# Tail scores of two pairs of heads in four 64x64 tiles, with a new order of the work: a fused attention and mixer kernel

## The chip, the core and the metric

The kernel runs on one core of one Trainium2 chip. Its time is device microseconds of one execution; the median of three runs of the kernel before is 616.5 us (616.19 to 616.97). Engines are named as in the profile: PE (TensorE matmul), PEld (its weight loads), DVE (VectorE), ACT (ScalarE), POOL (GpSimd) and SP (here the queue that issues the DMAs).

## The reference

Attention with rotary position embedding over 4 batches, 8 heads, 576 positions and 64 numbers per head, and then an MLP mixer on the result, all in float32:

```
q_rot, k_rot = rotate(q), rotate(k)
scores = matmul(q_rot, k_rot.T) / sqrt(64);  scores -= max(scores)
attn = exp(scores);  attn /= sum(attn) + 1e-9
x = matmul(attn, v), heads side by side              # (4, 576, 512)
u = x + (relu(x.T @ w_tok1) @ w_tok2).T              # mixing over the 576 positions
out = u + relu(u @ w_ch1) @ w_ch2                    # mixing over the 512 channels
```

The four mixer weights are float64 in memory.

## The kernel before

**Attention** goes pair by pair: 16 pairs of heads of one batch. 576 positions are 4 blocks of 128 and a tail of 64. `prep(n)` loads k, q and v of a pair (SP), rotates k and q (L339 to L345, on POOL; for the first pair on DVE), transposes them in 64x64 pieces on PE (L373) and copies them out of PSUM (L384). `pair(n)` takes the query blocks in `ORDER = [0, 1, None, 2, 3]`, where `None` is the tail. Per block of 128 queries:

- L467: scores of both heads, each as a 64x128 tile of PE (head 0 on rows 0 to 63, head 1 on rows 64 to 127, side by side), in two halves of 288 keys. A float32 matmul makes two records in the profile, so one half of one block is four records.
- L418: DVE scales the scores into SBUF and keeps the running extreme; L422: ACT takes the exponential over 576 keys and its sum.
- L490: PE transposes the probabilities, L495 copies them to `pt` (on ACT or DVE, as the planner finds; two copies per head).
- L508: after two blocks, probabilities times v, as two 128x64 column tiles; 256 columns for blocks 0 and 1, 320 for blocks 2, 3 and the tail. L511 copies it out, L537 transposes it back, L542 and L546 divide by the sums into X.

The **tail** of a pair has 64 queries for each of two heads. `prep` writes them as the two diagonal blocks of a 128x128 operand `bd` (L395, two POOL copies per pair; the rest of `bd` is zero), and L437 multiplies all 128 rows of k with it, in the whole array. Its sums stand in column R of `l`; L520 moves half of them to the lower partitions, L523 adds 1e-9 (POOL) and L526 inverts (DVE).

**Mixer weights** are turned from float64 into pairs of float32 parts by `f64_split` (L577 to L598), a chain that goes ACT, DVE, ACT, with some steps on DVE or POOL as the planner finds. `tokens(b)` splits X into two parts (L659, L661) and mixes the positions of batch b (first weights L679, relu L684 and L687, second weights L701, sum L704). Batch 0 is mixed inside the attention program, batches 1 to 3 in `mixers`. Then X is transposed (L770, L775, L776), and `cm1` (L796) and `cm2` (L819, sum L821) mix the channels in 4 groups of 5 chunks; the last sums go to memory.

**The order** of the work is not the order of the code. Every step is a `Task` of a `Plan` with an engine (or two to choose from), a guessed duration, what it needs, the buffers it holds and a priority. `Plan.run` gives each engine again and again the ready task with the lowest priority among those that could start within `SLACK` of the earliest; a task with two engines takes the one where it would end first. Priorities are 9 per pair plus the numbers of the table `AT`; `LAG` is the time from the end of a task to the start of one that needs it. The hardware sees only the order that comes out, with semaphores.

Of the kernel before, what the change touches and what calls it, by code (L numbers as in the profile page):

```python
# [65 lines left out]
class Task:  # L66
    __slots__ = ("alts", "deps", "bufs", "prio", "end", "eng", "waits", "heirs", "mode", "port", "lag")


LAG = {"PE": 0.2, "ACT": 0.14, "DVE": 0.12, "POOL": 0.12, "SP": 1.8}  # L70


class Plan:


    def __init__(self):
        self.tasks = []
        self.clock = {e: 0.0 for e in LAG}
        self.slack = SLACK
        self.mode = None  # L80

    def add(self, eng, dur, fn, deps=(), bufs=(), prio=0.0, alts=(), mode="full", port=False, lag=0.0):
        t = Task()
        t.mode = mode
        t.port = port
        t.lag = lag
# [38 lines left out]
    def run(self):  # L125
# [10 lines left out]
        while left:  # L136
            best = {}
            for t in ready:
                c = None
                for eng, dur, fn in t.alts:  # L140
# [4 lines left out]
                    if c is None or s + dur < c[0]:  # L145
                        c = (s + dur, s, eng, dur, fn)
# [3 lines left out]
            for eng, lst in best.items():  # L150
                first = min(x[0] for x in lst)
                x = min((x for x in lst if x[0] <= first + self.slack[eng]), key=lambda x: (x[1], x[0]))
                if pick is None or x[0] < pick[0]:
                    pick = x
            assert pick, "no task can start"
            t, (end, s, eng, dur, fn) = pick[2], pick[3]
# [36 lines left out]
AT = {'load': [-311.48, -308.58, -58.96], 'rot': [1889.94, -216.09], 'pt': [-100.67, -63.74], 'bd': [-253.52], 'qk': [14.66, 1777.02, -290.55, -143.73, -330.56, -75.94, -278.36, -253.03, -71.25, -216.26], 'mx': [28.88, 15.51, -498.29, -196.51, -331.08, 1812.6, -110.88, -411.67, -437.32, 1660.53, -65.25, 1592.69, -438.98, -224.08, -437.26, 1980.9, -38.01, -303.7, -400.95, -14.52], 'ex': [-299.71, 1566.3, 1763.5, 33.52, -329.21, -34.07, -105.55, -415.73, 1706.66, -38.02], 'tr': [23.38, -74.36, -44.78, 1659.9, -10.24, -95.08, 2000.17, 1899.59, -435.89, -250.66], 'cp': [-408.04, -310.8, -118.02, -449.87, -264.03, -245.16, -436.72, -414.97, -25.86, -38.07], 'pv': [1795.8, -117.48], 'p1': [1768.03, -101.8], 'fin': [2001.36], 'tok': [-4.78, 1596.11, -550.18, 17.36, 1868.43, 1586.91], 'inv': [1863.98], 'f6': [1766.06], 'tk': [11.25, 1893.27, -116.2, -80.72]}  # L193
EARLY = 1
FIRST = -60.0
SWITCH = 0.15
SLACK = {'PE': 0.018, 'ACT': 0.047, 'DVE': 0.002, 'POOL': 0.109, 'SP': 0.028}
# [18 lines left out]
def pool(n):  # L216
    return n * 0.00235 + 0.08
# [3 lines left out]
def rope_attention_mixer_kernel(ctx: ExitStack, tc: tile.TileContext, q, k, v, w_tok1, w_tok2, w_ch1, w_ch2, tab, out):  # L221
# [37 lines left out]
    def attention(ctx):  # L259
# [12 lines left out]
        bds = slots("bd", 3, [P, P])  # L272
# [4 lines left out]
        ls = slots("l", 4, [P, R + 1, 2])  # L277
        ris = slots("ri", 3, [P, R + 1, 2])
# [20 lines left out]
        ready, ready_v, bd_of = {}, {}, {}  # L299
# [5 lines left out]
        def prep(n):  # L305
            b, hp = divmod(n, HP)
            pos = 9 * n
            for nm, src, pr in (("k", k, 0.0), ("q", q, 0.5), ("v", v, 1.0)):
# [13 lines left out]

                pl = pos + AT["load"][int(2 * pr)]
                rows = ((0, 2), (2, R)) if n == 0 and nm == "k" else ((0, R),)
                l = [add("SP", 0.5, ld(*x), bufs=[rb], prio=pl) for x in rows]
                l += [add("SP", 0.65, (ldv if nm == "v" else ldt)(o), bufs=[rb], prio=pl) for o in range(2)]
# [26 lines left out]
                for r0, r1 in parts:  # L353
                    if r0:
                        x = x + l[1:]
                    for i in range(4):
# [4 lines left out]
                        else:  # L361
                            x = [add("POOL", pool(w * (z1 - z0) // (R + 1)), rot(nc.gpsimd, i, r0=z0, r1=z1), x, bufs, pos + AT["rot"][int(2 * pr)])
# [26 lines left out]
                if nm == "q":  # L389
                    bb = Buf(bds)  # L390
                    bdone = []
                    pp = pos + AT["bd"][0]
                    for h in range(2):
# [3 lines left out]
                    bd_of[n] = (bdone, bb)  # L397

        ORDER = [0, 1, None, 2, 3]
        W2 = S // 2  # L400

        def pair(n):
            b, hp = divmod(n, HP)
            lb = Buf(ls)
            pt = [Buf(pts) for _ in range(2)]
# [506 lines left out]
```

## Time and profile before

| | |
|---|---|
| median of three runs | 616.5 us (616.19 to 616.97) |
| profiled execution, span from the first to the last instruction | 614.2 us |
| what lies outside the span, against the median | 2.3 us |
| PE busy | 596.1 us, 97% |
| DVE, ACT, POOL busy | 439.8, 304.8, 220.0 us |
| granted PE clock | 1.00 |

The profiled execution has no time of its own beside its span, so the span is compared with the median. Read it in stages: up to 13 us the first operands arrive; from 13 to 265 us attention runs (PE, DVE, ACT and POOL all busy); from 265 to 312 us positions are mixed; from 312 us on channels are mixed, where PE goes on almost without a gap.

### The profile page before, as it was taken

The numbers are of one execution on the slowest core, as the hardware profiler recorded it, in microseconds if no ns is written. First come the engines' busy times: TensorE is split into PE (matmuls) and PEld (weight loads), VectorE is DVE, ScalarE is ACT, GpSimd is POOL, SyncE is SP. The second block draws the span as 40 slices with busy tenths as digits, with TensorE's granted clock in tenths as the row PEclk, the third lists the DMA queues.
The fourth block names the chain that finished last, engine by engine and source line by source line (L and its number), as shares of the span: only waits on it lengthen the run. The fifth ranks groups of instructions, "written<-read, shape, count | busy, mean of one in ns | idle before, by whom it ended". The sixth has DMA issues, their size and how long they took to land.

```text
span 614.2 us, 12749 instructions
## 1 busy us (share of the span) xinstructions
PE 596.1 (97%) x4752; PEld 465.6 (76%) x4752; DVE 439.8 (72%) x1243; ACT 304.8 (50%) x769; POOL 220.0 (36%) x347
## 2 busy tenths in 40 slices
PE   4999999999999999998999999999999999999997
PEld 3777777777677777766788888888888888888885
DVE  6899999999999999389779895388334943223232
ACT  2988998999788888435235542144102411011110
POOL 3989979888899710235221020001000000000000
PEclk9999999999999999999999999999999999999999
DMA  5622332323221020002122320042001200001123
GB/s 156 184 66 82 85 99 64 99 72 82 67 65 42 25 70 2 2 27 60 35 60 69 115 75 27 1 128 78 0 1 34 70 1 0 1 0 69 68 69 102
DMA packets 33676, 36.13 MB, mean 59 GB/s; under 512 B 13776, under 2 KB 27088, under 8 KB 33616
## 3 DMA queue, kind: packets, MB, share of 16 engines
q1 hardware_dynamic: 32784, 35.01, 19.7%
q8 instruction: 37, 0.61, 0.4%
q10 hardware_dynamic: 832, 0.33, 0.2%
q14 instruction: 23, 0.19, 0.1%
HBM read 30.61 MB, written 4.72 MB: 58 GB/s over the span
## 4 chain that ended last, share of the span: by engine, by line
PE 90%; DVE 6%; DMA 1%; ACT 1%; issue 1%; ACTq 0%; POOL 0%; DVEq 0%; SPq 0%; POOLq 0%
PE m L796 24%; PE m L819 24%; PE s L508 11%; PE s L467 10%; PE s L490 6%; PE m L701 3%; PE s L437 3%; PE m L679 2%; PE s L373 2%; DVE p L418 1%; PE s L701 1%; PE s L679 1%; PE s L447 1%; PE s L537 1%; DVE xs L661 1%
## 5 line engine op out<-in xcount | busy, mean ns | idle before, releaser
L798 ACT ACTIVATE gh<-m 128x512 fp32r<-128x512 f32 (+1 forms) x60 | 33.3, 555 | 173.9 <-PE m L796 173.6
L422 ACT ACTIVATE p<-p,nm 128x576 f32<-128x576 f32 x128 | 98.4, 772 | 18.8 <-DVE p L418 18.3
L800 DVE SCALAR_TENSOR_TENSOR gl<-m,gh 128x512 fp32r<-128x512 f32 (+1 forms) x60 | 38.3, 638 | 70.0 <-ACT gh L798 69.6
L796 PE MATMUL m<-uh,c1h 128*128 128x512 f32 (+1 forms) x240 | 88.4, 368 | 0.0
L796 PE MATMUL m<-ul,c1h 128*128 128x512 f32 (+1 forms) x240 | 88.3, 368 | 0.0
L796 PE MATMUL m<-uh,c1l 128*128 128x512 f32 (+1 forms) x240 | 88.3, 368 | 0.0
L821 DVE TENSOR_TENSOR X<-m,X 128x512 f32<-128x512 f32 x64 | 44.2, 690 | 57.6 <-PE m L819 57.1
L508 PE MATMUL s<-pt,vraw 128*64 128x256 f32 (+1 forms) x640 | 84.8, 411 | 0.0
L819 PE MATMUL m<-c2h,gh 128*128 128x512 f32 x216 | 84.2, 390 | 0.0
L819 PE MATMUL m<-c2l,gh 128*128 128x512 f32 x216 | 84.1, 389 | 0.0
L819 PE MATMUL m<-c2h,gl 128*128 128x512 f32 x216 | 84.0, 389 | 0.0
L467 PE MATMUL s<-kt,qt 64*128 64x288 f32 x512 | 82.7, 430 | 1.0 <-DVE qt L384 0.7
L508 PEld LDWEIGHTS s<-pt,vraw 128*64 128x64 f32 x640 | 43.6, 137 | 32.3 <-DVE p L418 2.3
L589 POOL TENSOR_TENSOR fa<-fc,fa 128x384 f32<-128x384 f32 (+3 forms) x13 | 13.3, 1020 | 138.6 <-DVE fa L587 138.6
L418 DVE TENSOR_SCALAR_CACHE_REDUCE p<-s,nm 128x288 f32<-128x288 f32 x128 | 61.2, 511 | 0.5 <-PE s L467 0.3
L490 PEld LDWEIGHTS s<-ident,p 64*128 64x128 f32 x1152 | 48.7, 139 | 14.5 <-issue 4.5
L467 PEld LDWEIGHTS s<-kt,qt 64*128 64x128 f32 x512 | 50.5, 192 | 9.8 <-DVE p L418 1.7
L490 PE MATMUL s<-ident,p 64*128 64x64 f32 x1152 | 55.0, 226 | 0.9 <-DVE oT L511 0.4
L418 DVE TENSOR_SCALAR_CACHE_REDUCE p<-s 128x288 f32<-128x288 f32 x128 | 53.3, 450 | 2.2 <-PE s L467 1.9
L495 ACT COPY pt<-s 128x320 f32<-128x320 f32 (+1 forms) x146 | 52.0, 411 | 4.4 <-PE s L490 3.6
L796 PEld LDWEIGHTS m<-ul,c1h 128*128 128x128 f32 x240 | 45.2, 189 | 7.7
L796 PEld LDWEIGHTS m<-uh,c1h 128*128 128x128 f32 x240 | 45.2, 188 | 7.7
(135 smaller groups left out, 1080.5 us busy)
## 6 DMA issues: line engine op xcount, KB each, us to landing
stg<-in_moe_w_ch_dram SPq DMA_DIRECT2D x16, 384.0 KB, 3.2
stg<-in_moe_w_ch_dram SPq DMA_DIRECT2D x12, 512.0 KB, 3.7
qraw<-in_q_dram SPq DMA_DIRECT2D x16, 256.0 KB, 2.9
vraw<-in_v_dram SPq DMA_DIRECT2D x16, 256.0 KB, 2.8
out_dram<-X SPq DMA_DIRECT2D x16, 256.0 KB, 2.3
kraw<-in_k_dram SPq DMA_DIRECT2D x15, 256.0 KB, 2.8
stg<-in_moe_w_tok_dram SPq DMA_DIRECT2D x4, 512.0 KB, 4.4
kraw<-in_k_dram SPq DMA_DIRECT2D x32, 32.0 KB, 2.6
```

Source lines behind the costliest of these rows:

```text
L418: return lambda: nc.vector.tensor_scalar(out=p()[:, c * W2:(c + 1) * W2], in0=sb.t[:, 0:W2], scalar1=-D ** -0.5, scalar2=nm.t[:, 0:1] if c ...
L422: return lambda: nc.scalar.activation(out=p(), in_=p(), func=ACTF.Exp, bias=nm.t[:, 1:2], scale=-1.0, accum_out=l())
L467: nc.tensor.matmul(sbs[h].t[:, 0:W2], flat(qt.t)[halves[h], TL + j * P:TL + (j + 1) * P], flat(kt.t)[halves[h], TL * (1 - h) + u * W2:TL * ...
L490: nc.tensor.transpose(xy[z].t[:, i * TL:(i + 1) * TL], pb.t[halves[z], c0:c0 + P], ident[halves[z], halves[z]])
L495: return lambda: e(out=pt[c].t[:, R * h:R * h + m, o + z * TL:o + (z + 1) * TL], in_=xy[z].t[:, 0:m * TL].rearrange("p (r s) -> p r s", r=m))
L508: nc.tensor.matmul(ab.t[halves[h], 0:w], vb.t[:, h, r, :], m, start=(r == 0), stop=(r == R))
L701: nc.tensor.matmul(tb.t[0:w], a, m, start=(i == 0), stop=(i == 5))
L796: nc.tensor.matmul(tb.t[:, 0:n], a, m, start=(i == 0), stop=(i == len(lst) - 1))
L798: x = add("ACT", act(n), lambda f=f, tb=tb: nc.scalar.activation(out=gb.t[0][:, f, 0:n], in_=tb.t[:, 0:n], func=ACTF.Relu), [x], [tb, gb], ...
L800: y = add("DVE", dve(n), lambda f=f, tb=tb: nc.vector.scalar_tensor_tensor(out=gb.t[1][:, f, 0:n], in0=tb.t[:, 0:n], scalar=0.0, in1=gb.t[ ...
L819: nc.tensor.matmul(tb.t, a, m, start=(i == 0), stop=(i == len(lst) - 1))
L821: y = add("DVE", 0.69, lambda u=u, tb=tb: nc.vector.tensor_tensor(out=u, in0=tb.t, in1=u, op=ALU.add), [z] + sums.get((ci, x), []), [tb], ...
```

## The change

- **Tail scores.** `bd` and its copies are gone. `tails(n)` does the tails of two pairs n and n+1 (n even) together: four matmuls of 64 rows by 64 columns, each on its own quarter of the array (64 queries of one head of one pair against 288 keys), in a fourth mode `quad` beside row, col and full. Head h goes to PSUM bank h, so one bank holds the two pairs' queries of one head. The tails stand fourth in the even pair and not at all in the odd one: `ORDER = ([0, 1, 2, None, 3], [0, 1, 2, 3])`.
- **What hangs on it.** The odd pair's tail columns go with its blocks 0 and 1, so its 320 wide product is the first and not the second. Tail sums have their own small tiles: `l` shrinks to 8 columns, one copy (L463), one addition (L464) and one reciprocal (L465) per two pairs come in for the tails, the copy L520 per pair goes.
- **The planner's numbers.** `LAG` gets new values and `PAIR` values by pair of engines; a choice between two engines adds `BIAS` (0.08 for DVE, -0.51 for POOL) to the end; priorities differ for even and odd pairs; `AT` and `SLACK` are new, also for the mixing of positions.
- **Smaller edits.** The first q is loaded in two parts like the first k; the splits of two row blocks of batch 1 move into the attention program (`PRE`); the last block's second product and sum go in two halves of 256 columns, each with its own DMAs out.

The core of the diff (the table `AT` is all new, two entries stand for it):

```diff
-LAG = {"PE": 0.2, "ACT": 0.14, "DVE": 0.12, "POOL": 0.12, "SP": 1.8}
+LAG = {"PE": 0.2, "ACT": 0.15, "DVE": 0.14, "POOL": 0.2, "SP": 2.4}
+PAIR = {("PE", "DVE"): 0.27, ("DVE", "PE"): 0.175, ("DVE", "ACT"): 0.115, ("ACT", "PE"): 0.16, ("POOL", "PE"): 0.52}
...
-                    if c is None or s + dur < c[0]:
-                        c = (s + dur, s, eng, dur, fn)
+                    key = s + dur + BIAS.get(eng, 0.0)
+                    if c is None or key < c[0]:
+                        c = (key, s, eng, dur, fn)
...
-AT = {..., 'pv': [1795.8, -117.48], ...}
+AT = {..., 'pv': [-52.61, -86.6, -9.66, -21.02], ...}
+PRE = 2
+BIAS = {'DVE': 0.08256, 'POOL': -0.51382}
...
-                        def cp(h=h, tb=tb, bb=bb):
-                            nc.gpsimd.tensor_copy(out=bb.t[halves[h], halves[h]], in_=tb.t[halves[h], 2 * R + 1])
-                        bdone.append(add("POOL", 0.3, cp, done, [bb, tb], pp))
...
-        ORDER = [0, 1, None, 2, 3]
+        ORDER = ([0, 1, 2, None, 3], [0, 1, 2, 3])
...
+                def qk(sbs=sbs, u=u):
+                    for x in range(2):
+                        for h in range(2):
+                            nc.tensor.matmul(sbs[h].t[halves[x ^ h], 0:W2], flat(qt[x].t)[halves[h], 2 * R * TL + TL:2 * R * TL + 2 * TL],
+                                             flat(kt[x].t)[halves[h], TL + u * W2:TL + (u + 1) * W2], start=True, stop=True)
+                x = add("PE", 0.485, qk, kd + qd + [x[0] for x in t], [*sbs, *kt, *qt, *nms_, *pbs], g + AT["qk"][2 * i + u], mode="quad")
...
-                            nc.tensor.matmul(sb.t[:, 0:W2], bb.t, flat(kt.t)[:, TL + u * W2:TL + (u + 1) * W2], start=True, stop=True)
-                        t = add("PE", 0.485, qk, bdone + kd + [t], [sb, bb, kt, nm, pb], g + AT["qk"][2 * i + u])
...
-                w = 2 * P + (TL if c == 1 else 0)
-                c0 = 2 * P * c
+                w = 2 * P + (TL if c != odd else 0)
+                c0 = c * (2 * P + odd * TL)
...
+                last = g == NG - 1 and ci == NC - 1 and x == len(chunks[ci]) - 1
+                w = DM // (2 if last else 1)
...
+            splits(EARLY, range(PRE), 9 * 4 * (EARLY + 1) + AT["pre"][0])
```

What comes out of the planner is shown at three places.

PE, in the middle of attention, before: from the transposes of one pair to its tail scores (L437) and its first product with v (L508).

```order
L490 MATMUL s<-ident,p_116 128x64 x18
L447 MATMUL s<-ident,pq_119 128x64 x10
L467 MATMUL s<-kt_109,qt_111 128x288 x8
L537 MATMUL s<-ident,oT_124 128x64 x10
L437 MATMUL s<-kt_109,bd_114 128x288 x2
L508 MATMUL s<-pt_123,vraw_103 64x256 x10
L373 MATMUL s<-ident,uk_105 128x64 x10
```

The same place in the changed kernel: L425 are the tail scores of two pairs, L502 and L525 the scores and transposes of blocks, L543 the product with v.

```order
L525 MATMUL s<-ident,p_112 128x64 x8
L425 MATMUL s<-kt_108,qt_110 64x288 x2
L425 MATMUL s<-kt_109,qt_111 64x288 x2
L425 MATMUL s<-kt_108,qt_110 64x288 x2
L425 MATMUL s<-kt_109,qt_111 64x288 x2
L525 MATMUL s<-ident,p_112 128x64 x10
L502 MATMUL s<-kt_108,qt_110 128x288 x2
L502 MATMUL s<-kt_109,qt_111 128x288 x4
L502 MATMUL s<-kt_108,qt_110 128x288 x2
L525 MATMUL s<-ident,p_113 128x64 x8
L543 MATMUL s<-pt_120,vraw_104 64x256 x10
```

Two full-array matmuls in each pair, most often right ahead of a product with v, became eight small ones in every second pair, both halves in one run between transposes; k and q of both pairs have to be there for them.

POOL, before, from the last rotation (L345): L395 the last copies for `bd`, L598 a low part of the position weights (the last step of `f64_split`; L589 and L591 are its product and sum), L523 additions to the sums, L661 splits of X.

```order
L345 TENSOR_TENSOR uq_106<-uq_106,w_107 128x6x32
L395 COPY bd_112<-qt_111 64x64 x2
L598 TENSOR_TENSOR w2l<-fh_70,w2h 128x512
L523 TENSOR_SCALAR l_128<-l_128 128x10
L523 TENSOR_SCALAR l_129<-l_129 128x10
L523 TENSOR_SCALAR l_130<-l_130 128x10
L661 TENSOR_TENSOR xs_87<-X_60,xs_87 128x512
L661 TENSOR_TENSOR xs_88<-X_60,xs_88 128x512
```

POOL in the changed kernel, from its last rotation (L352): L626, L628 and L635 are product, sum and low part, L555 and L464 the additions to the sums.

```order
L352 TENSOR_TENSOR uq_106<-uq_106,w_107 128x6x32
L628 TENSOR_TENSOR fh_70<-fh_70,fa_68 128x512
L555 TENSOR_SCALAR l_125<-l_125 128x8
L635 TENSOR_TENSOR w1l<-fh_69,w1h 128x512
L635 TENSOR_TENSOR w1l<-fh_70,w1h 128x512
L464 TENSOR_SCALAR lt_132<-lt_132 64x4
L555 TENSOR_SCALAR l_126<-l_126 128x8
L626 TENSOR_TENSOR fa_67<-fc,fa_67 128x256
L628 TENSOR_TENSOR fh_69<-fh_69,fa_67 128x256
L626 TENSOR_TENSOR fa_68<-fc,fa_68 128x512
L628 TENSOR_TENSOR fh_70<-fh_70,fa_68 128x512
L635 TENSOR_TENSOR w2l<-fh_70,w2h 128x512
```

Before, one 512 wide step of the position weights stood here and most others on DVE, in the middle of attention; now six stand in these rows, and two more in the next eight.

PE, in the mixing of positions, before: the first weights of batch 2 (L679), all second weights of batch 1 (L701), then the first weights of batch 2 again.

```order
L679 MATMUL m_4127<-xs_88,w1h 128x512 x2
L679 MATMUL m_4127<-xs_88,w1l 128x512
L701 MATMUL m_4121<-rs,w2h 128x512 x2
L701 MATMUL m_4121<-rs,w2l 128x512
L701 MATMUL m_4121<-rs,w2h 128x512 x2
L701 MATMUL m_4121<-rs,w2l 128x512
L701 MATMUL m_4122<-rs,w2h 128x512 x2
L701 MATMUL m_4122<-rs,w2l 128x512
```

The same place in the changed kernel: L724 are first weights, L746 second weights.

```order
L746 MATMUL m_4130<-rs,w2h 128x512 x2
L746 MATMUL m_4130<-rs,w2l 128x512
L724 MATMUL m_4134<-xs_88,w1h 128x512 x2
L724 MATMUL m_4134<-xs_88,w1l 128x512
L724 MATMUL m_4135<-xs_88,w1h 128x512 x2
L724 MATMUL m_4135<-xs_88,w1l 128x512
L724 MATMUL m_4134<-xs_87,w1h 128x512 x2
L724 MATMUL m_4134<-xs_87,w1l 128x512
L724 MATMUL m_4135<-xs_87,w1h 128x512 x2
L724 MATMUL m_4135<-xs_87,w1l 128x512
L746 MATMUL m_4131<-rs,w2h 128x512 x2
L746 MATMUL m_4131<-rs,w2l 128x512
```

Second weights of one batch and first weights of the next now alternate.

## Rows read from the trace of the kernel before

**Rows 1.** The page's parts 1 and 4: busy time; the chain by engine.

```profile
PE 596.1 (97%) x4752; PEld 465.6 (76%) x4752; DVE 439.8 (72%) x1243; ACT 304.8 (50%) x769; POOL 220.0 (36%) x347
...
PE 90%; DVE 6%; DMA 1%; ACT 1%; issue 1%; ACTq 0%; POOL 0%; DVEq 0%; SPq 0%; POOLq 0%
```

**Rows 2.** Stages: us, PE, PEld, DVE, ACT, POOL busy (instructions), clock, DMA share, GB/s.

```profile
13.00:265.00 252.00, 249.37 (x3042) 179.49 (x3038) 230.66 (x859) 210.04 (x590) 185.16 (x298) 1.00 0.25 69
265.00:312.00 47.00, 44.27 (x239) 33.70 (x240) 38.79 (x66) 16.91 (x32) 16.35 (x12) 1.00 0.14 40
312.00:614.20 302.20, 298.05 (x1448) 249.16 (x1447) 163.07 (x299) 75.44 (x141) 14.37 (x12) 1.00 0.16 49
```

**Rows 3.** The same view, stretches inside attention.

```profile
60.00:100.00 40.00, 39.48 (x494) 28.57 (x490) 39.35 (x145) 36.61 (x105) 35.49 (x57) 1.00 0.31 87
100.00:140.00 40.00, 39.91 (x511) 28.82 (x512) 39.71 (x146) 37.31 (x106) 35.29 (x58) 1.00 0.31 82
140.00:180.00 40.00, 39.59 (x518) 28.65 (x518) 39.08 (x146) 33.74 (x97) 35.07 (x58) 1.00 0.26 71
...
220.00:265.00 45.00, 44.10 (x452) 31.18 (x448) 31.06 (x107) 27.08 (x73) 5.96 (x6) 1.00 0.01 1
```

**Rows 4.** The chain that ended last, in time: start us, length us, what.

```profile
160.12 1.17 PE s L437 x4
161.29 2.31 PE s L508 x20
...
165.47 1.51 PE s L467 x12
167.23 2.84 PE s L508 x20
...
171.10 0.54 PE s L467 x4
...
175.56 2.31 PE s L508 x20
```

**Rows 5.** Groups, 13 to 265 us: shapes xcount | busy us, mean ns.

```profile
L495 ACT COPY pt<-s 128x320 f32<-128x320 f32 x87 | 35.1, 432 | 3.9 <-PE s L490 3.3
L495 DVE COPY pt<-s 128x256 f32<-128x256 f32 x69 | 27.4, 415 | 0.7 <-PE s L490 0.5
...
L495 ACT COPY pt<-s 128x256 f32<-128x256 f32 x59 | 21.3, 380 | 0.5 <-PE s L490 0.3
...
L495 DVE COPY pt<-s 128x320 f32<-128x320 f32 x41 | 19.6, 478 | 0.1
```

**Rows 6.** The same view: tail copies, and steps of the weights on both engines.

```profile
L395 POOL COPY bd<-qt 64x64 f32<-64x64 f32 x32 | 8.5, 266 | 14.0 <-ACT qt L384 9.1 <-DVE qt L384 3.0 <-PE s L490 1.0
...
L589 DVE TENSOR_TENSOR fa<-fc,fa 128x512 f32<-128x512 f32 x4 | 4.7, 1182 | 0.0
...
L598 POOL TENSOR_TENSOR w2l<-fh,w2h 128x512 fp32r<-128x512 f32 x1 | 1.5, 1542 | 1.1 <-ACT w2h L597 1.1
```

**Rows 7.** Line L345: duration ns min/median/max, first and last start us.

```profile
L345 POOL TENSOR_TENSOR uq<-uq,w x30: 445/584/1062, 22.5 to 212.1; 128x128 f32<-128x128 f32 x15, 128x192 f32<-128x192 f32 x15
```

**Rows 8.** The chain again, mixing of positions.

```profile
244.21 6.68 PE s L679 x28
...
263.68 0.56 DVE XT L704
...
286.06 2.31 DVE xs L661 x2
288.37 2.23 DVE ul L776 x4
...
304.30 0.70 DVE rs L687
```

**Rows 9.** The chain's end.

```profile
597.78 12.28 PE m L819 x54
610.09 0.69 DVE X L821
```

More of the change, by code (lines that the diff above doesn't have):

```diff
@@ L194 @@
 EARLY = 1
+PRE = 2
 FIRST = -60.0
-SWITCH = 0.15
-SLACK = {'PE': 0.018, 'ACT': 0.047, 'DVE': 0.002, 'POOL': 0.109, 'SP': 0.028}
+SWITCH = 0.1
+SLACK = {'PE': 0.01443, 'ACT': 0.01454, 'DVE': 0.05146, 'POOL': 9.226190723928434e+32, 'SP': 0.028}
+BIAS = {'DVE': 0.08256, 'POOL': -0.51382}
 def act(n, sbuf=False):
@@ L321, in ldv @@
                     return lambda: nc.sync.dma_start(out=rb.t[halves[o], o, R, :], in_=a[o, M:S])
[L323 to L326, printed above, removed]
+                pl = pos + AT["load"][3 * odd + int(2 * pr)]
+                parts = n == 0 and nm != "v"
+                rows = ((0, 2), (2, R)) if parts else ((0, R),)
+                first = lambda r0: 10 * FIRST + pr + r0 if parts else pl
+                l = [add("SP", 0.5, ld(*x), bufs=[rb], prio=first(x[0])) for x in rows]
+                l += [add("SP", 0.65, (ldv if nm == "v" else ldt)(o), bufs=[rb], prio=first(2)) for o in range(2)]
                 if nm == "v":
@@ L402, in pair @@
+        tail_inv, pts_of, ev_of = {}, {}, {}
         def pair(n):
             b, hp = divmod(n, HP)
+            odd = n % 2
             lb = Buf(ls)
-            pt = [Buf(pts) for _ in range(2)]
+            if not odd:
+                for m in (n, n + 1):
+                    pts_of[m] = [Buf(pts) for _ in range(2)]
+                    ev_of[m] = {0: [], 1: []}
+                    couple[m] = (pts_of[m][1 - m % 2], ev_of[m][1 - m % 2])
+            pt, ev = pts_of[n], ev_of[n]
             kp, kt = ready[n, "k"]
@@ L459, in pair @@
+                    tail_inv[n] = tail_inv[n + 1] = tails(n, g, i)
                     continue
@@ L649, in rope_attention_mixer_kernel, with splits @@
     u_done = {}
-    def tokens(b, banks):
-        px, p1, p2, p3 = [9 * 4 * (b + 1) + z for z in AT["tk"][4 * b:4 * b + 4]] if b < EARLY else [10.0 * b + z for z in (0, 1, 1.5, 2)]
-        sp = []
-        for r in range(R + 1):
+    split = {}
+    def splits(b, rows, px):
+        for r in rows:
             xb = Buf(xss if r < R else xts)
@@ L659, in tokens @@
             c = lambda e, hi=hi, src=src: lambda: (e.copy if e is nc.scalar else e.tensor_copy)(out=hi(), in_=src)
-            x = add("ACT", act(DM, True), c(nc.scalar), x_done[b], [xb], px, alts=[("DVE", dve2(DM), c(nc.vector))])
+            x = add("ACT", act(DM, True), c(nc.scalar), x_done[b], [xb], px, port=True, alts=[("DVE", dve2(DM), c(nc.vector))])
             f = lambda e, hi=hi, lo=lo, src=src: lambda: e.tensor_tensor(out=lo(), in0=src, in1=hi(), op=ALU.subtract)
-            y = add("DVE", dve(DM), f(nc.vector), [x], [xb], px, alts=[("POOL", pool(DM), f(nc.gpsimd))] if r < R else [])
-            sp.append((xb, [x, y]))
+            y = add("DVE", dve(DM), f(nc.vector), [x], [xb], px, port=True, alts=[("POOL", pool(DM), f(nc.gpsimd))] if r < R else [])
+            split[b, r] = (xb, [x, y])
+    def tokens(b, banks):
+        if b < EARLY:
+            px, p1, p2, p3 = [9 * 4 * (b + 1) + z for z in AT["tk"][4 * b:4 * b + 4]]
+        else:
+            px, p1, p2, p3 = AT["tm"][4 * (b - EARLY):4 * (b - EARLY) + 4]
+        splits(b, [r for r in range(R + 1) if (b, r) not in split], px)
+        sp = [split[b, r] for r in range(R + 1)]
         rb = Buf(rss)
@@ L832, in mixers @@
             tokens(b, m_ps)
-        held = weights(0, 25, (1,))
+        for r in range(PRE):
+            split[EARLY, r][0].users -= 1
+        held = weights(0, AT["wg"][0], (1,))
         held[0].users += 1
         for ci in range(2):
-            ups[ci] = up(ci, 12 + ci)
+            ups[ci] = up(ci, AT["up"][ci])
         plan.run()
@@ L862, in rope_attention_mixer_kernel @@
                 tokens(b, banks)
+            splits(EARLY, range(PRE), 9 * 4 * (EARLY + 1) + AT["pre"][0])
+            for r in range(PRE):
+                split[EARLY, r][0].users += 1
             plan.run()
```

218 lines of the change are left out of this document (119 added, 99 removed).

## The prediction

> **What bounds the kernel now.** I read the page's busy line and chain first: PE is busy for 97% of the span and holds 90% of the chain that ended last; DVE holds 6%, nearly all that is left [rows 1]. Then the stages: 13 to 265 us is attention, 265 to 312 us the mixing of positions, and the 302 us behind it the mixing of channels, where PE is busy for 298 us and the change touches two instructions' worth of work [rows 2]. So the gain or loss has to come from the first 312 us.
>
> Then the stretches inside attention: a PE that is called full does 494, 511 or 518 matmuls in 40 us, so a few per cent are slack even there. In the 120 us from 60 to 180 DVE is busy for 39.35 + 39.71 + 39.08 = 118.1 us, ACT for 36.61 + 37.31 + 33.74 = 107.7 us, POOL for 105.9 us; at the end of attention (220 to 265 us) POOL is almost idle, 6 of 45 us, and DVE has 14 us free [rows 3]. The reader is to see a PE with three helpers close behind it: what PE saves counts only as far as DVE and ACT can follow.
>
> **Tail scores.** The block-diagonal product of a pair is four records and 1.17 us of the chain; 16 pairs make 18.7 us [rows 4]. In its place come, for two pairs, two runs of four tiles with 288 columns in two passes. No row shows four tiles at once. Two tiles side by side do 288 columns twice in 1.51 / 3 = 0.50 us (scores, row tiles); the products with v, also two tiles, take 2.31 / 10 = 0.231 us for a pass of 256 columns and 2.84 / 10 = 0.284 us for 320, so about 0.258 us for 288 [rows 4]. If four tiles go as two do, two runs cost 2 x 0.50 = 1.0 us, or 4 x 0.258 = 1.03 us. To this comes entering and leaving the mode: the 1.17 us of the old block hold 1.0 us for its four passes, so 0.17 us for one extra change, and the new block stands between transposes and changes twice; I take 0.3 us. So 1.3 us for two pairs instead of 2.34, 1.04 us saved, 8 times: 8.3 us off PE. Bounds: two tiles at a time cost 2.0 + 0.3 us and save nothing (0.3 us over 8 couples); one tile at a time costs 16 passes x 0.25 + 0.3 = 4.3 us, 2.0 us more than before, 8 times: +16 us. I take the upper end, because both rows nearest to it, row tiles and column tiles, show that a second tile costs no time of its own.
>
> The Trainium skill, TensorE: Matmul & The Clock Gate, section Part 3: Packing small matmuls, says that a pack lasts as long as one of its matmuls and some 4 ns for each further tile, in rows and columns alike; by that the block costs the same 1.3 us. No run here shows it for four tiles.
>
> The wait that the change adds: tails of pair n now need k and q of pair n+1, and behind them in PE's row stand the rest of pair n's blocks and its second product. Before, PE already did scores of the next pair ahead of a pair's second product, so the operands are there; only for the first couple nothing covers it. There, and for the first q in two parts (one DMA more on SP), I put +0.5 us, between 0 and 1.5.
>
> **Work that changes engines.** Counted in the order of both programs, 47 of the 110 copies of probabilities on DVE go to ACT, 33 of 256 and 14 of 320 columns. DVE loses 33 x 0.415 + 14 x 0.478 = 20.4 us; ACT gains 33 x 0.380 + 14 x 0.432 = 18.6 us [rows 5]. Of the other copies nine come to ACT and nine go. POOL loses the 32 copies for the block-diagonal operand, 8.5 us, and gets the wide steps of the position weights that took DVE 1.18 us each in attention and take POOL 1.54 us [rows 6]. Most stand behind its last rotation.
>
> So DVE is relieved and ACT becomes the second engine. Attention can give back the 8.3 us only where ACT follows. Its 210.0 us become 228.6 us [rows 2, 5]. In the middle 120 us that is 107.7 + 18.6 x 120 / 252 = 116.5 us; if ACT gets as full as DVE was, 118.1 of 120, the stretch can shrink to 118.4 us: 1.6 us. In the other 132 us ACT has 102.4 + 9.7 = 112.1 us and is no bound, so these give their part, 8.3 x 132 / 252 = 4.3 us. Together -5.9 us; bounds 0 (ACT holds everything) and -11 (8.3 us, and in the stretch with 494 matmuls another 40 x 24 / 518 = 1.9 us, since DVE no longer carries weights there, and 1 us more of the same kind).
>
> On that, a second place of the Trainium skill speaks against the new cover: SBUF — State Buffer, Who interferes with whom, says that a DVE instruction with two inputs in SBUF and a POOL instruction that reads SBUF exclude each other. The trace agrees that something does: the DVE step with two SBUF inputs took 1.18 us, the sum with one input in PSUM, as wide, 0.69 us [rows 6, 9]. By that rule the steps left on DVE may each wait for a POOL step of 1.54 us at the end of attention, where DVE has 14 us free [rows 3, 6]; the sum above would stay.
>
> **Mixing of positions.** The chain from 263.68 to 304.30 us holds eight pieces over 0.5 us that are not PE, together 9.1 us; the two longest are the split of X and the low part of the transposed X, both on DVE [rows 8]. A low part of the channel weights (1.28 us of the eight) goes from DVE to POOL, and with first weights of one batch and second weights of the next alternating, the relu pair that ends at 304.30 us plus 0.70 (1.31 us of them) has matmuls beside it. Splits and low parts stay, though three more casts are on ACT: 0.4 us. I take -3.0 us; between 0 and -7.
>
> **The rest.** The two halves of the last block: the last sum of 0.69 us [rows 9] works on half the columns, some 0.26 us less, and PE does 18 short matmuls for 9 long ones, some 0.12 us more: -0.1 us, at most 0.3 either way. POOL's slower steps of the channel weights have 302 us with 14 us of work in them [rows 2]: 0; if a group's weights came late, PE would show a gap there. Loads keep their number but for the one of q.
>
> **Sum.** +0.5 - 5.9 - 3.0 - 0.1 = -8.5 us on the profiled span of 614.2 us: 605.7 us. The median of the runs lies 2.3 us above the span; with the same 2.3 us the time is 608.0 us.
>
> **Rivals.**
> - ACT holds attention where it is. For: the middle would need ACT at 116.5 of 120 us, and its work waits on DVE in between. Against: ACT has over 30 us free outside it. Then only -3.0 - 0.1 + 0.5 are left: 613.9 us.
> - Four tiles go as two pairs, the change doesn't do what it says. Attention gains 0.3 us from PE and about 1 us from DVE's relief: 0.5 - 1.3 - 3.0 - 0.1 = -3.9, 612.6 us. Against it is that two tiles of either kind are free.
> - POOL is late at the seam. Behind its last rotation (in the trace before it starts at 212.1 us) it now has eight wide steps, 8 x 1.54 = 12.3 us, and some narrow ones, and the first weights are wanted at 244.21 us [rows 6 to 8]. There is room, but the steps alternate with DVE and ACT; if the last block's three steps are waited for, that is 3 x 1.54 = 4.6 us: 612.6 us.
> - Slower: the tiles are served one after the other. One mechanism, at every one of the 8 blocks, 2.0 us more than the two blocks that went; from 2.34 us per block on the change loses. +16 us on PE, which nothing hides, with -3.0 - 0.1 + 0.5: 629.8 us. For it is only that no row shows the mode.
>
> **Chances.** Forecast 0.69 (its own range 603 to 612 us); ACT 0.13; pairs of tiles 0.06; seam 0.07; one by one 0.05. A difference under 0.2%, 1.2 us, is about what a measurement of this kernel cannot tell from none; that line is at 615.3 us. All of the forecast lies below it, and of ACT, pairs and seam, whose centres are 612.6 to 613.9 us, some 0.17 of 0.26 lie below and 0.08 within 0.2%. So faster 0.86, same 0.08, slower 0.06. The range of 602 to 614.5 us takes in the forecast and half of the rivals on its upper side.
>
> **What would show it.** Right: the eight records of a block of tail scores start in fours a few ns apart, a block takes about 1.3 us of the chain; attention ends some 5 us earlier; ACT is the busiest engine beside PE from 60 to 180 us, over 38 of 40 us, and DVE falls below 37; the pieces that are not PE between attention and the mixing of channels sum to about 6 us. Wrong: a block of 2 us or 4 us; POOL as releaser of the first weights; ACT named before PE for several us in the middle of attention; or a mixing of channels that is longer than 302 us, which no step above expects.

## The result, and the profile after

The changed kernel takes 611.26 us (median of four runs, 610.55 to 612.06) where the kernel before, run beside it, takes 616.74 us (616.19 to 617.11): ratio 0.9913, 95% interval 0.9899 to 0.9927, 5.5 us less. The forecast was 608.0 us with a range of 602 to 614.5 us: the direction and the range held, the gain was 5.5 us where 8.7 us (616.7 - 608.0) were forecast. That the number came out this near is in part luck: two steps of the sum were each wrong by more than the 3.2 us that the whole is off, with opposite signs.

The page's busy line and the chain by engine, of the changed kernel, answer to [rows 1]:

```profile
PE 589.5 (97%) x4825; PEld 462.5 (76%) x4825; DVE 392.5 (64%) x1128; ACT 317.1 (52%) x814; POOL 294.4 (48%) x387
...
PE 75%; ACT 17%; DVE 4%; issue 2%; DMA 1%; POOL 0%; DVEq 0%; ACTq 0%; SPq 0%
```

DVE is 47 us emptier, POOL 74 us fuller, and ACT holds 17% of the chain where it held 1%.

The stages, cut where each kernel's own chain leaves attention and starts the mixing of channels (columns as in [rows 2]): first the changed kernel, then the kernel before, whose third stage is in [rows 2].

```profile
13.00:253.10 240.10, 235.51 (x3064) 169.56 (x3062) 204.95 (x801) 216.50 (x622) 182.13 (x279) 0.99 0.27 73
253.10:305.30 52.20, 50.64 (x280) 39.53 (x280) 38.75 (x64) 22.28 (x42) 22.10 (x18) 1.00 0.12 36
305.30:608.60 303.30, 298.82 (x1457) 250.22 (x1456) 141.41 (x241) 75.23 (x141) 85.24 (x71) 1.00 0.16 49
```

```profile
13.00:256.60 243.60, 241.87 (x3003) 173.95 (x2999) 226.58 (x852) 206.41 (x583) 179.69 (x294) 1.00 0.26 71
256.60:312.00 55.40, 51.77 (x279) 39.25 (x280) 42.87 (x72) 20.54 (x39) 21.82 (x16) 1.00 0.12 34
```

Attention ends 3.5 us earlier, the mixing of positions gives 3.2 us, the mixing of channels costs 1.1 us: 5.6 us on the span. And the mean granted clock in attention is 0.99, not 1.00.

Inside attention the two kernels differ far more than these 3.5 us. A couple of pairs (two pairs, whose tails are now done together) has four products with v. Timeline of PE, the fourth product and the 28th, six couples later, first in the kernel before:

```profile
45.20 2.91 PE L508 MATMUL s<-pt,vraw 128*64 128x320 f32 x20
...
225.72 2.91 PE L508 MATMUL s<-pt,vraw 128*64 128x320 f32 x20
```

```profile
55.81 2.38 PE L543 MATMUL s<-pt,vraw 128*64 128x256 f32 x20
...
223.82 2.38 PE L543 MATMUL s<-pt,vraw 128*64 128x256 f32 x20
```

The fourth product ends at 48.1 us before and at 58.2 us in the changed kernel: 10.1 us later. The 28th ends at 228.6 and 226.2 us, so the six couples between took 30.1 us each before and take 28.0 us each now: 12.5 us less. Some of both is order. At 58.2 us the changed kernel has more scores and transposes of later pairs behind it than the kernel before has at 48.1 us (104 and 170 records for 90 and 144, and 82 for 70 of k and q); at the second mark it is 488 and 1036 for 480 and 1028, and 320 of k and q in both. With these records priced by the chain, an estimate is that the start costs about 7 us and the middle gives between 10 and 11 us.

**The tail scores cost a little less than was forecast.** Timeline of PE, the block of the second couple (the last couple's, at 220.00 us, takes the same 1.20 us):

```profile
51.99 1.20 PE L425 MATMUL s<-kt,qt 64*64 64x288 f32 x16
```

In the trace the 16 records of such a block start in fours, at 0, 7, 13 and 20 ns; the second four start 0.29 us after the first, the others 0.24 us after the four ahead of them. (The first couple's block at 26.74 us does not start in such fours.) The Trainium skill (TensorE: Matmul & The Clock Gate, section Part 3: Packing small matmuls) has a pack last as long as one of its matmuls plus some 4 ns for each further tile. The trace agrees that the four run side by side, with 7 ns from one to the next. In the chain a block takes 1.13 us, where 1.3 us were forecast:

```profile
192.15 1.13 PE s L425 x16
```

For 16 blocks of 1.17 us [rows 4] stand 8 of 1.13 us: 9.7 us off PE. In the six couples of the middle that is 12 x 1.17 - 6 x 1.13 = 7.3 us, so tail scores are most of what the middle gives, and some 3 us of it come from the rest of the new order. From the second couple's block to the last one's, six couples later, it is 168.0 us: again 28.0 us for two pairs.

**The start gives much of it back.** The same view as [rows 3], first the start of the changed kernel in steps of 2 us, then its timeline on PE:

```profile
18.00:20.00 2.00, 0.00 (x0) 0.00 (x0) 0.55 (x3) 2.00 (x7) 2.00 (x4) 0.62 0.53 151
20.00:22.00 2.00, 1.94 (x36) 1.94 (x38) 0.92 (x2) 1.26 (x5) 2.00 (x4) 0.50 0.47 150
22.00:24.00 2.00, 2.00 (x22) 1.36 (x20) 0.92 (x2) 1.27 (x4) 2.00 (x3) 0.50 0.66 185
24.00:26.00 2.00, 2.00 (x16) 1.13 (x12) 0.00 (x0) 0.00 (x0) 2.00 (x6) 0.67 0.83 254
```

```profile
16.16 0.87 PE L380 MATMUL s<-ident,uk 64*128 64x64 f32 x10
20.06 2.72 PE L525 MATMUL s<-ident,p 64*128 64x64 f32 x46 [3.04 <-ACT p L406]
22.71 3.64 PE L543 MATMUL s<-pt,vraw 128*64 128x256 f32 x20
```

PE waits 3.04 us for an exponential. While it stands idle, at about 18.5 us, the granted clock falls to 0.50, the 1.2 GHz level, and stays there until about 25.3 us: the product of 256 columns takes 3.64 us, where the one at 55.81 us takes 2.38 us. The Trainium skill (the same page, section Part 1: The HAM clock gate) says that a PE that idles is clocked at half speed and gets the full clock back only after work; the trace agrees, and the forecast had not priced it. What PE waits for is a matter of order: ACT runs through its six exponentials and two copies almost without a gap, and the one that PE needs is the last. ACT's order at this place:

```
L406 ACTIVATE p0_112,l0_124<-p0_112,nm0_135 128x576
L406 ACTIVATE p1_113,l0_124<-p1_113,nm2_137 128x576
L530 COPY pt0_118<-s_143 128x4x64 x2
L406 ACTIVATE p2_114,l0_124<-p2_114,nm5_140 128x576
L406 ACTIVATE p1_113,l0_124<-p1_113,nm3_138 128x576
L406 ACTIVATE p2_114,l0_124<-p2_114,nm4_139 128x576
L406 ACTIVATE p0_112,l0_124<-p0_112,nm1_136 128x576
```

The second head of block 0 (`nm1`) comes last of six, and in PE's order its transposes come second.

**In the middle** (the same view, answering to [rows 3]) DVE is relieved and ACT busier, as forecast, but ACT stays under 38 of 40 us where over 38 were forecast, and DVE is at 37.04 us in one stretch where less than 37 was:

```profile
60.00:100.00 40.00, 39.81 (x546) 29.13 (x542) 35.76 (x145) 36.80 (x110) 35.04 (x54) 1.00 0.29 75
100.00:140.00 40.00, 39.77 (x554) 28.78 (x552) 37.04 (x143) 37.22 (x108) 32.27 (x50) 1.00 0.28 74
140.00:180.00 40.00, 39.81 (x567) 29.52 (x565) 34.66 (x141) 37.45 (x114) 33.05 (x53) 1.00 0.28 72
```

ACT is busy for 111.5 of these 120 us; the forecast had 116.5. Even so the chain names ACT for several us at a time in the middle of each couple, which the forecast had listed as a sign of being wrong; one of these pieces (the others are alike):

```profile
60.04 3.14 ACT p L406 x8
```

So a reader of the chain alone could take ACT for the engine that holds the middle. Runs 3 and 4 ask which one does.

### The profile page after: what moved, and what is told of

Same layout as the page of the kernel before. It is cut to its first block, busy times and chain, and to the rows that moved or that the text cites. A ratio compares the mean times of both kernels' runs of the same rounds, so it can differ in the third digit from the quotient of the medians.

```text
span 608.6 us, 12892 instructions
## 1 busy us (share of the span) xinstructions
PE 589.5 (97%) x4825; PEld 462.5 (76%) x4825; DVE 392.5 (64%) x1128; ACT 317.1 (52%) x814; POOL 294.4 (48%) x387
## 4 chain that ended last, share of the span: by engine, by line
PE 75%; ACT 17%; DVE 4%; issue 2%; DMA 1%; POOL 0%; DVEq 0%; ACTq 0%; SPq 0%
PE m L841 24%; PE m L868 24%; ACT p L406 8%; PE s L543 7%; PE s L502 5%; PE s L525 4%; ACT pt L530 4%; PE m L746 3%; PE m L724 2%; ACT pq L406 1%; PE s L746 1%; PE s L380 1%; ACT pt L453 1%; PE s L724 1%; ACT pt L457 1%
## 5 line engine op out<-in xcount | busy, mean ns | idle before, releaser
L543 PE MATMUL s<-pt,vraw 128*64 128x256 f32 (+1 forms) x640 | 85.7, 415 | 0.0
L868 PE MATMUL m<-c2h,gh 128*128 128x512 f32 (+1 forms) x219 | 84.7, 387 | 0.1
L868 PE MATMUL m<-c2l,gh 128*128 128x512 f32 (+1 forms) x219 | 84.6, 386 | 0.0
L868 PE MATMUL m<-c2h,gl 128*128 128x512 f32 (+1 forms) x219 | 84.6, 386 | 0.0
L502 PE MATMUL s<-kt,qt 64*128 64x288 f32 x512 | 83.9, 430 | 0.5 <-ACT qt L391 0.5
L870 DVE TENSOR_TENSOR X<-m,X 128x512 f32<-128x512 f32 (+1 forms) x65 | 44.4, 683 | 61.0 <-PE m L868 60.4
L530 ACT COPY pt<-s 128x320 f32<-128x320 f32 (+1 forms) x193 | 66.2, 414 | 8.9 <-PE s L525 8.5
L626 POOL TENSOR_TENSOR fa<-fc,fa 128x384 f32<-128x384 f32 (+3 forms) x31 | 35.0, 1129 | 64.8 <-DVE fa L624 57.0
L525 PEld LDWEIGHTS s<-ident,p 64*128 64x128 f32 x1152 | 49.9, 142 | 21.3 <-ACT p L406 6.2
L543 PEld LDWEIGHTS s<-pt,vraw 128*64 128x64 f32 x640 | 43.7, 138 | 29.3 <-issue 1.9
L402 DVE TENSOR_SCALAR_CACHE_REDUCE p<-s,nm 128x288 f32<-128x288 f32 x128 | 62.7, 513 | 2.8 <-ACT qt L391 0.9
L525 PE MATMUL s<-ident,p 64*128 64x64 f32 x1152 | 56.8, 230 | 3.9 <-ACT p L406 3.0
L502 PEld LDWEIGHTS s<-kt,qt 64*128 64x128 f32 x512 | 51.3, 194 | 7.0 <-ACT qt L391 0.7
```

The lines of the kernel that those rows point to most:

```text
L402: return lambda: nc.vector.tensor_scalar(out=p()[:, c * W2:(c + 1) * W2], in0=sb.t[:, 0:W2], scalar1=-D ** -0.5, scalar2=nm.t[:, 0:1] if c ...
L502: nc.tensor.matmul(sbs[h].t[:, 0:W2], flat(qt.t)[halves[h], TL + j * P:TL + (j + 1) * P], flat(kt.t)[halves[h], TL * (1 - h) + u * W2:TL * ...
L525: nc.tensor.transpose(xy[z].t[:, i * TL:(i + 1) * TL], pb.t[halves[z], c0:c0 + P], ident[halves[z], halves[z]])
L530: return lambda: e(out=pt[c].t[:, R * h:R * h + m, o + z * TL:o + (z + 1) * TL], in_=xy[z].t[:, 0:m * TL].rearrange("p (r s) -> p r s", r=m))
L543: nc.tensor.matmul(ab.t[halves[h], 0:w], vb.t[:, h, r, :], m, start=(r == 0), stop=(r == R))
L626: mul_ = lambda e: lambda: e.tensor_tensor(out=A(), in0=C(), in1=A(), op=ALU.mult)
```

## The experiments

Runs 1 to 8, 10 and 11 issue the planned order again with a few tasks exchanged or added, so that the rest of the program stays as it was. Runs 9 and 12 go through the planner again; in run 12 only the moved splits changed their place, in run 9 the order changed all over attention. The edits are shown in short form. Line numbers are those of each run's own kernel. Ratios are to the kernel before, run beside each; differences to the changed kernel are between medians, and a kernel's times spread over 1 to 5 us.

**1. The start: exponentials in order**

```diff
+CHAINS = [[ex(0,h0), ex(0,h1), copies(0,h0), ex(1,h0), ex(1,h1), ex(2,h0), ex(2,h1)], [the DVE steps ahead of them, block by block]]
```

> The changed kernel with one reordering in the first pair: ACT's six exponentials, and DVE's steps ahead of them, stand block by block, so that the second head of block 0, for which PE waits 3.04 us from 17.0 us on, comes second and no longer last. Theory A (the start gives back what attention gains: the wait, and the clock at 1.2 GHz behind it from 19 to 25 us): the first product with v starts near 20.5 us and not at 22.78, at full clock, and the time falls by 3 to 5 us, to 606 to 608 us. Theory B (ACT holds attention, as the forecast had it): ACT's work is the same, so the time stays within 1 us of 611.3 us.

Measured: 608.70 us, ratio 0.9873 (0.9859 to 0.9886), 2.6 us less than the changed kernel. PE's longest wait between 9 and 60 us is 0.8 us and no longer 3.0, and the clock is 1.00 over the whole profiled execution. The first product with v starts at 21.5 us, not at 20.5, and the gain is below what theory A expected. The chain says what was late next:

```profile
22.59 4.60 DMA stg<-in_moe_w_tok_dram
27.21 0.68 ACT fa L671
27.89 0.57 ACT fc L673
28.46 0.74 ACT pq L460 x2
```

ACT's order has a step of the position weights (L671) ahead of the tails' exponentials (pq); ACT stands idle for 1.96 us until the load of these weights lands at 27.2 us. No run moved this step.

**2. The start: the wait filled**

```diff
+for _ in range(6 if n == 0 and j == 0 and h == 1 else 0):
+    nc.tensor.matmul(xy[0].t[:, 0:W2], <64 rows of q>, <288 columns of k>, start=True, stop=True)
```

> The changed kernel with six extra matmuls of 288 columns on PE (2.9 us, their result is overwritten) in the place where PE waits 3.04 us for an exponential. The wait stays as long. Theory A with the clock as a cost of its own: the granted clock stays 1.00 from 18 to 26 us, the 45 transposes take 1.4 us and not 2.72, the first product 2.31 us and not 3.57, and the time falls by about 2.6 us to 608.7 us. If the clock costs nothing in the end, because ACT or POOL hold what follows: 611.3 us within 0.8 us.

Measured: 609.14 us, ratio 0.9879 (0.9863 to 0.9895), 2.1 us less. PE's timeline:

```profile
16.05 3.17 PE L533 MATMUL s<-kt,qt 64*128 64x288 f32 x12
19.36 1.66 PE L537 MATMUL s<-ident,p 64*128 64x64 f32 x46
20.96 2.75 PE L555 MATMUL s<-pt,vraw 128*64 128x256 f32 x20
```

The same transposes take 1.66 us for 2.72, the same product 2.75 us for 3.64. The tails start at 24.10 us and not at 26.74; 2.0 of these 2.6 us are the clock (1.06 on the transposes, 0.89 on the product), 0.7 us are exponentials that end earlier in this execution. So the clock is worth most of what run 1 gained. In the profiled execution of this run the clock fell at another place instead, after three waits of PE between 322 and 324 us that sum to 0.9 us:

```profile
324.00:326.00 2.00, 1.86 (x9) 1.44 (x6) 2.00 (x4) 2.00 (x6) 1.23 (x2) 0.53 0.02 4
```

**3. Who holds the middle: PE doubled**

```diff
-                    for x in range(2):
+                    for x in (0, 1, 0, 1):
```

> The changed kernel with every run of four tail tiles issued twice (the same values written again): two passes of 0.24 us more per run, two runs per two pairs, 8 times: 7.8 us more on PE. Theory A (PE holds the middle of attention, 27.9 of 28 us): the time rises by 6 to 8 us, to 617 to 619 us. Theory B (ACT holds it): by less than 2 us, under 613.3 us.

Measured: 617.17 us, ratio 1.0009 (0.9999 to 1.0019), 5.9 us more. Second and last block:

```profile
53.60 2.17 PE L435 MATMUL s<-kt,qt 64*64 64x288 f32 x32
...
227.37 2.17 PE L435 MATMUL s<-kt,qt 64*64 64x288 f32 x32
```

The block grows by 0.97 us and two pairs take (227.37 - 53.60) / 6 = 28.96 us, 0.96 us more: in the middle PE time that is added counts in full. The 5.9 us lie at the lower edge of what theory A expected, far from theory B's; ACT, with the same work, does not hide any of it. With the saving on the tails given back, the kernel is no faster than the kernel before.

**4. Who holds the middle: more on ACT**

```diff
+more = lambda e, z=z, xy=xy: e == nc.scalar.copy and e(out=spare, in_=xy[z].t[:, 0:R * TL])
```

> The changed kernel with 31 extra copies on ACT, 256 columns each (0.38 us, into a spare tile that nobody reads), one behind each tail copy that ACT does: 11.8 us more on ACT, 1.5 us per two pairs. Theory A (PE holds the middle, ACT has 1.9 of 28 us free per two pairs): the time rises by 0 to 4 us, to 611 to 615 us. Theory B (ACT holds it): by 9 to 12 us, to 620 to 623 us.

Measured: 618.25 us, ratio 1.0018 (1.0009 to 1.0028), 7.0 us more, between the two expectations.

```profile
51.58 1.20 PE L436 MATMUL s<-kt,qt 64*64 64x288 f32 x16
...
225.36 1.20 PE L436 MATMUL s<-kt,qt 64*64 64x288 f32 x16
```

Two pairs take 28.96 us: of 1.5 us more on ACT, 1.0 us shows and 0.5 us is hidden. So ACT stands some 0.5 us behind PE per two pairs: it does not hold the middle, but it leaves little room, though in the changed kernel it is idle for 2.6 to 3.2 of 40 us. It also says that a further saving on PE would soon stop paying; that was not run.

**5 to 7. The kernel before, PE or DVE relieved**

```diff
-nc.tensor.matmul(sb.t[:, 0:W2], bb.t, flat(kt.t)[:, TL + u * W2:TL + (u + 1) * W2], ...)
+nc.tensor.matmul(sb.t[:, 0:W2 // 2], bb.t, flat(kt.t)[:, TL + u * W2:TL + u * W2 + W2 // 2], ...)
```

> The kernel before, with only the first 144 of the 288 columns of each half of the tail scores computed (the rest of those scores is left out): 16 pairs x 4 passes x 0.12 us = 7.7 us less on PE, and nothing else moved. Theory P (PE alone held attention in the kernel before): the time falls by 6 to 8 us, to 609 to 611 us. Theory C (DVE, busy for 39.3 of 40 us, held its middle): by less than 3 us, 614 us or more.

```diff
+for 47 of the 110 copies planned on DVE: issue it on ACT at the same place
```

> The kernel before, its order kept, with 47 of DVE's 110 copies of probabilities done by ACT at the same place: 20 us less on DVE, 18 us more on ACT, PE unchanged. Theory C (DVE held the middle): the time falls by 3 to 6 us, to 611 to 614 us. Theory P (PE alone): within 1.2 us of 616.7 us.

> The kernel before with both edits at once: half of the tail scores' columns left out (7.7 us less on PE, alone -2.7 us) and 47 of DVE's copies on ACT (alone +1.9 us). If the two only add, as two edits in an order that was made for neither: 616.7 - 2.7 + 1.9 = 615.9 us, within 1.2 us. Theory D (PE and DVE hold attention together, and only relief of both pays): below 612 us.

Runs 5 and 7 leave out half of the columns of the tail scores. Measured: PE relieved 614.08 us (ratio 0.9960, 0.9942 to 0.9977); DVE relieved 618.68 us (1.0032, 1.0020 to 1.0044), slower, where theory C expected a gain; both 616.41 us (1.0004, 0.9995 to 1.0013). The chain of the first, and the same place in the chain of the kernel before:

```profile
152.06 1.25 DVE p L428 x6
153.30 1.14 DVE w2l L608
154.44 0.62 DVE fa L591
...
155.52 0.52 PE s L500 x9
```

```profile
154.45 1.40 DVE w2l L598
```

In the old order 7.7 us less on PE bring 2.7 us, for at such places the chain goes through DVE, which makes position weights (L608, L598 before) between the scores. But taking copies off DVE without a new order brings a loss. ACT, busy for 36.6 and 37.3 of 40 us from 60 to 140 us in the kernel before, is then busy for 38.0 and 38.8; that it does the copies at a place where it has other work is argued, not shown. Both edits together give no more than the two apart: -2.7 + 1.9 = -0.8 us, measured +0.1. Theory P and theory D fall; theory C holds for the place of the wait (DVE) and falls for the remedy.

**8. The mixing of channels: weights on DVE again**

```diff
+    for x in seq:
+        if x[0] in ONE and x[1] == "POOL":      # second channel weights of group 0
+            x[1:] = [(e, fn) for e, dur, fn in x[0].alts if e == "DVE"][0]
```

> The changed kernel, its order kept, with the 11 steps that make the second channel weights of the first group done by DVE and not by POOL at the same place (0.69 to 1.0 us each for 1.3 to 1.9 us). Theory A (these weights come 1.1 us too late at 326.3 us, and PE waits there, at times with the clock at 1.2 GHz behind it): the mixing of channels takes 302.2 us and not 303.3 us, and the time falls by 1 to 2 us, to 609.3 to 610.3 us. Rival (DVE is the one that is late there, with eight parts of the transposed X): within 0.6 us of 611.3 us, or slower.

Measured: 611.69 us, ratio 0.9915 (0.9902 to 0.9929): no difference. The waits on PE in this stretch, changed kernel and this run:

```profile
PE m L815 <- DVE ul L821: 0.8, 3, 0.3
```

```profile
PE m L832 <- DVE ul L838: 1.4, 3, 0.7
```

The transposes of X wait for the low parts that DVE makes of them, and more so when DVE makes weights too. The rival holds as far as the run goes: no wait of PE in this stretch names POOL in either kernel. But the edit takes work off POOL and puts it on DVE, so it cannot tell whether POOL alone would have cost nothing.

**9. The start: block 3 ahead of the tails**

```diff
-            for i, j in enumerate(ORDER[odd]):
+            for i, j in ((0, 0), (1, 1), (2, 2), (4, 3), (3, None)) if n == 0 else enumerate(ORDER[odd]):
```

> The kernel of the run with the exponentials in order, and in the first pair block 3 ahead of the tails and not behind them; the planner makes a new order from this, so steps move elsewhere in attention too. Theory A (the rest of what the start loses, some 3 us between 9 and 40 us, comes from the tails that wait for the second pair's operands while PE has nothing else): the first two pairs end 1 to 3 us earlier than at 56.1 us, and the time falls from 608.7 us to 606 to 607.5 us. Rival (ACT's eight exponentials in a row hold the start): the first two pairs end where they did, and the time is 608 us or more.

Measured: 637.32 us, ratio 1.0341 (1.0328 to 1.0355). The planner laid out all of attention anew, and PE's two longest waits are

```profile
PE s L582 <- ACT p L460: 8.4, 5, 4.6
PE s L434 <- DVE uk L406: 7.3, 2, 5.1
```

where the changed kernel's longest is 3.0 us. So the run does not tell the two theories apart. What it shows: the table fits one program, and one step exchanged under it made a plan that takes 28.6 us more than run 1.

**10. The start: the product first**

```diff
+CHAINS = [[ex(0,h0), ex(0,h1), copies, ex(1,h0), ex(1,h1), copies of blocks 0 and 1 in between, ex(2,h0), ex(2,h1)], [tr(1,h1), pv(0), tr(2,h0), tr(2,h1)]]
```

> The kernel of the run with the exponentials in order, and besides that in the first pair the first product with v ahead of block 2's transposes on PE, and the copies that it needs ahead of block 2's exponentials on ACT. Theory A (what the start still loses against the kernel before is PE's wait for ACT, where these copies stood behind six exponentials): the first product starts near 20.3 us and not at 21.5 us, and the time falls by 1 to 2 us, from 608.7 us to 606.7 to 607.7 us. Rival (the second pair's rotations on POOL, which run without a gap until 31 us, hold the start): 608.7 us within 0.8 us.

Measured: 608.83 us, ratio 0.9877 (0.9864 to 0.9891), the same as run 1.

```profile
19.22 0.65 PE L603 MATMUL s<-pt,vraw 128*64 128x256 f32 x2 [0.39 <-ACT pt L589]
20.63 2.44 PE L603 MATMUL s<-pt,vraw 128*64 128x256 f32 x18 [0.76 <-ACT pt L589]
...
24.87 1.74 PE L483 MATMUL s<-kt,qt 64*64 64x288 f32 x16
```

The product starts 2.3 us earlier than in run 1, and the tails behind it stand where they stood (24.7 us there). PE waits for ACT's copies instead. Theory A falls for this part; that POOL holds it, as the rival has it, is not shown either. The chain goes through the load of the position weights here too (4.70 us from 22.36 us on). So the step on ACT that waits for this load, ahead of the tails' exponentials, is the next suspect in both runs; it was not moved.

**11. Copies back to DVE**

```diff
+for 47 of the 193 copies planned on ACT: issue it on DVE at the same place
```

> The changed kernel, its order kept, with 47 of ACT's 193 copies of probabilities done by DVE at the same place: about 20 us less on ACT and as much more on DVE, PE unchanged. Theory E (the copies had to leave DVE for PE to run at 27.9 us per two pairs; DVE would be busy for 27 of 28 us): the time rises by 3 to 6 us, to 614 to 617 us. Rival (PE alone holds attention, ACT and DVE both have room): within 1.2 us of 611.3 us.

Measured: 616.99 us, ratio 1.0016 (1.0005 to 1.0027), 5.7 us more, as theory E expected. Two pairs take (225.13 - 52.51) / 6 = 28.77 us:

```profile
52.51 1.54 PE L444 MATMUL s<-kt,qt 64*64 64x288 f32 x16
...
225.13 1.54 PE L444 MATMUL s<-kt,qt 64*64 64x288 f32 x16
```

In this order the new pace needs the copies on ACT. But DVE is busy for 26.1 of 28 us here (68 to 208 us), not for 27, and run 6 lost 1.9 us by the opposite move, also in an order that was kept, so a part of the loss can come from moving copies without planning anew; whether DVE could carry them in an order of their own was not run.

**12. Splits not moved**

```diff
-PRE = 2
+PRE = 0
```

> The changed kernel with PRE = 0: the splits of two row blocks of batch 1 stay in the mixing of positions, as in the kernel before. Theory F (their place inside attention is a part of the 3 us that the mixing of positions gave): the first weights of batch 1 start later, and the time rises by 1 to 2 us, to 612.3 to 613.3 us. Rival (the wait behind attention is set by the last sums of batch 0 and the transposes, which are there either way): within 0.8 us of 611.3 us.

Measured: 610.12 us, ratio 0.9901 (0.9883 to 0.9919), which is not apart from the changed kernel. Theory F falls: no gain of the moved splits shows.

## Why the prediction was right, and where it was not

- **Tail scores, -8.3 us on PE: right in its mechanism.** Four tiles go as one, a block costs 1.13 us for 1.3 forecast, and 9.7 us come off PE. Run 3 shows that PE time counts in the middle: with it put back the gain is gone. The rivals of two tiles at a time and of one at a time are out.
- **The start, +0.5 us: too cheap, by 6 to 7 us.** PE's wait of 3.04 us and the slow clock behind it (2.72 for 1.66 us, 3.64 for 2.75 us: 2.0 us, by run 2) are 5 us in two rows; the estimate for the whole start is 7 us. The forecast looked for operands that come late (k and q of the second pair) and not for the place of an exponential in ACT's order, though the order shows it. Run 1 got 2.6 us back and run 2 2.1 us; these overlap, for both keep the clock up. What holds the rest is open; the chains of runs 1 and 10 name the load of the position weights and the steps on ACT behind it.
- **ACT caps the gain of 8.3 us at 5.9 us: wrong.** The step took a busy share like DVE's of before for a limit, and let the 120 us from 60 to 180 us shrink by 1.6 us. The products of two pairs went from 30.1 to 28.0 us, 8 us in 120. ACT's load in it was too large: 18.6 us more were forecast, and in attention (13 us to its end in each kernel) ACT is busy for 216.5 us after 206.4. The 47 copies did move (193 copies for 146), but lengths were added, and ACT's records overlap (an exponential starts at 17.64 us and lasts 0.76 us, the next record starts at 18.31 us). And the forecast let attention gain at most what the tails save; the some 3 us that the rest of the new order gave in the middle stood in its lower bound alone. In run 3 the middle follows PE one for one. ACT is close, though: from 0.5 us more per two pairs it decides (run 4). The rival that ACT holds attention where it was is out.
- **So the sum was near by luck in attention:** 3.5 us were gained where 5.9 - 0.5 = 5.4 us were forecast. The start cost about 7 us and not 0.5, the rest gave between 10 and 11 us and not 5.9; the two errors have opposite signs.
- **DVE's relief: needed in this order, and not sufficient.** With the copies back the gain is gone (run 11, with its reservation). In the old order neither PE's saving nor the moved copies bring it (runs 5 to 7: 2.7, -1.9 and none). So the gain belongs to the new order with both. Which of the planner's new numbers carries it was not tried.
- **Mixing of positions, -3.0 us: right in size, 3.2 us; in its reasons half.** The waits of PE from the end of attention on, before and in the changed kernel:

```profile
PE m L770 <- DVE XT L546: 1.4, 1, 1.4
PE m L679 <- DVE xs L661: 1.2, 1, 1.2
PE m L701 <- DVE rs L687: 0.7, 2, 0.4
PE m L701 <- ACT rs L684: 0.3, 1, 0.3
```

```profile
PE m L724 <- DVE XT L749: 0.8, 1, 0.8
PE m L724 <- DVE xs L698: 0.6, 1, 0.6
```

  The wait for the relu pair (rs) has gone, as forecast. The waits for the transposes (XT) and for the split (xs), which the forecast left as they were, shrank by 1.2 us; no run took this apart, and the splits that moved into attention had no part that shows (run 12). The pieces of the chain that are not PE and over 0.5 us sum to 7.8 us (forecast: about 6), for one came in that the forecast did not have, 2.9 us for a load of channel weights.
- **The rest, -0.1 us: +1.1 us.** The mixing of channels got longer, which the forecast listed as a sign that no step of it expects; it named POOL's channel weights as what could cause a gap there. The waits name DVE's low parts of X instead (0.8 us), and run 8 does not speak against it. The halved last sum does what was forecast: the last piece of the chain is 0.42 us for 0.69 us [rows 9].
- **POOL late at the seam** (the change from attention to the mixing of positions): the chain names POOL once there, for 0.25 us. The rival is out.

The fastest version that was run is the changed kernel with the first pair's exponentials in order, 608.70 us, 1.3% under the kernel before.

## What to carry to other kernels

When an edit brings a new order, read the first microseconds apart from the steady part: the same table of priorities serves both, and at the start one instruction late in one queue can idle TensorE and cost its clock as well. Price a wait on TensorE at its length plus the slow work that can follow (here 3.0 and 2.0 us). A saving on the busiest engine is paid out only in an order that fits the others too: 7.7 us less on PE were worth 2.7 us in the old order. And when a total comes out near the forecast, compare its stages: here two errors had hidden each other.

## What was not expected of the hardware

In the changed kernel the granted clock fell to the 1.2 GHz level 1.4 us into a wait of PE of 3.04 us and came back 5.3 us after PE had work again. Early in the mixing of channels, between 322 and 333 us, three waits that sum to 0.8 or 0.9 us were followed by a drop to the same level in the profiled executions of runs 2, 10, 11 and 12 (in run 2: 0.53 and 0.62 granted in the two stretches from 324 to 328 us) and not in those of the changed kernel and of runs 1, 3 and 4, which have the same three waits. Executions of one program differ in their mean clock: four runs of the changed kernel have 0.994, 0.994, 0.991 and 0.991 with spans of 608.6, 609.0, 610.1 and 609.7 us.
